# A routed expert kernel: the last group's row scatters lose their index copies, and in three-tile visits the next visit's rows are transposed one unit later

## The chip, the core and the metric

The kernel runs on one core of one Trainium2 chip. The metric is the device time of one execution in microseconds; lower is better. The engines that matter are PE (matrix multiply; PEld is its weight load), ACT and DVE (elementwise work), POOL (here mostly the issue of indirect DMAs) and SP (the issue of plain DMAs). They run from separate instruction queues, each in order, and wait for one another through semaphores. All DMAs of the core share 16 DMA engines.

## The reference

A convolution over 7 neighbouring positions with softmax weights makes 23040 token rows of 192 values. Each row is then routed to one of 4 groups and one of 4 experts in that group, goes through that expert's two-layer network, and is scaled.

```python
w = np.exp(weight_gen - max); w = w / (w.sum(-1) + 1e-9)         # B=8, S=2880, H=8, K=7
x = np.einsum('bshk,bskhg->bshg', w, x_unf).reshape(23040, 192)
g_idx = argmax(x @ w_group)                                       # 4 groups
e_idx = argmax(xg @ w_expert[g])                                  # 4 experts in each
h = np.maximum(xg @ w1[g, e], 0.0)                                # 192 -> 1024
out[tok] = g_w * e_w * (h @ w2[g, e])                             # 1024 -> 192
```

## The kernel before

The tokens pass in 15 groups of 12 x 128. For each group DVE makes the convolution, and the router gives each token a row number `posi` in a buffer `rows` in device memory, where each expert has a stretch of its own. `scatter_row` (L522) writes 128 rows of 194 values at a time with an indirect DMA that POOL issues, 12 of them a group (L527).

In the groups of `SPACED` each scatter first copies its 128 row numbers from `posi` into one of three small tiles `ix` (L526, a ring of three). A copy may run only when the scatter that last used its tile is done, so that no more than about three scatters are under way. In groups outside `SPACED` the scatter reads `posi` directly.

After the last group `table` also writes 16 fills of 256 padding rows (L599, `rows<-rem`), one for each expert's end. The results of the experts go out by indirect DMAs on the same POOL queue (L1049, `out<-y`). The order of POOL's instructions is set when the program is built, and POOL follows it strictly.

The experts' work is a list of visits: one visit loads one expert's weights and runs 1, 2 or 3 tiles of 128 rows through it (a cut visit has two and a half, or one and a half). A visit of two tiles has 4 units, a visit of three (`cur.wide`) has 8. The main loop of `blocks` (L1176) emits for each unit, in this order: the first product `gemm1` of unit u; for some u the preparation of the next visit; the second product `gemm2` of two units before, and after a visit's last unit `finish`, with its output copies `y` (L1038, ACT), and for cut visits `gemm2_half` (16 small products, L1022).

The preparation of the next visit `nxt` is `prep_x(nxt, 0)`: four transposes of two row tiles on PE into the tile `tpx` (L939, L940), a copy on ACT that rounds them (`xh`, L945), and on DVE the remainder (`xl`, L896, as all the delayed subtractions). When the next visit has a third tile, `prep_x(nxt, 2)` comes at unit 4, and in a three-tile visit it uses the same `tpx`, so it waits until `xl` has read it. Before the transposes ACT copies the last 64 columns of the rows to `xd` (L921).

Weights come in by SP: the first layer's as three loads into `raw` (L848, L855), the second layer's as one load of 768 KB (L859). In the round of six two-tile visits before the last round, and in the last round, the second layer is split into two parts: ACT rounds it to `wc` in two halves (L888), DVE makes the remainders, and there is a single `raw` buffer for it, so that the next load starts when the second half is done. In these visits DVE also makes the remainder of each hidden unit (`pr`, L896 as SCALAR_TENSOR_TENSOR), after ACT's `hh` (L979) and, in cut visits, ACT's copy of the half tile (L983).

The last round of visits, which needs the last group's rows, has 3 visits of three tiles, 7 of two and a half, 2 of two, 4 of one and a half and 2 of one. One further visit of three tiles stands in an earlier round, and there the second layer is not split.

Of the kernel before, what the change touches and what calls it, by code (L numbers as in the profile page):

```python
# [22 lines left out]
LATE = (1.0, 3.0, 3.0)  # L23
AHEAD = (1.0, 1.0, 2.5)
HURRY = 12
SPACED = range(2, 15)
HALVES = (36.0, 42.0, 48.0, 54.0, 60.0, 66.0, 72.0, 78.0)
WHOLE = 12
SINGLE = tuple((k,) for k in range(7))
# [13 lines left out]
def conv_moe_kernel(ctx: ExitStack, tc: tile.TileContext, x, wgen, w_group, w_expert, w1, w2, out):  # L43
# [221 lines left out]
    def run(eng, cost, *deps):  # L265
        clk[eng] = max([clk[eng]] + [d + HOP for d in deps]) + cost
        return clk[eng]
# [10 lines left out]
    def round_of(g):  # L278
        return next(r for r in range(NR) if g < ENDS[r])
# [170 lines left out]
    def ranks(g, o, ls, tls):  # L450
# [64 lines left out]
        for s in range(n):  # L515
            run("pool", 2.2 if g in SPACED else 1.28, clk["dve"])
            scatter_row(pi[:, s:s + 1], xrow[s // SC][:, s % SC, :], round_of(g), g in SPACED)
        if g + 1 in ENDS:
# [3 lines left out]
    def scatter_row(idx, src, r, spaced):  # L522
        ix = idx
        if spaced:
            ix = new_ix()
            nc.gpsimd.tensor_copy(out=ix, in_=idx)  # L526
        written_once(nc.gpsimd.indirect_dma_start(  # L527
            out=rows[:, :], out_offset=bass.IndirectOffsetOnAxis(ap=ix, axis=0),
            in_=src, in_offset=None, bounds_check=NROW - 1, oob_is_err=False), r)
# [272 lines left out]
    def ready(n):  # L802
        return order[n][:2] in arrive

    def plain(n):
        return order[n][1] == 1
# [101 lines left out]
    def flush():  # L908
        for q in (late, held):
            while q:  # L910
                q.pop(0)()
        held.extend(later)
        later[:] = latest
        latest.clear()

    def prep_d(b):
        if b.plain:
            return
        b.xd = new_xd()[:, 0:b.nt]
        b.td = run("act", 0.1 + 0.13 * b.nt, b.o.tx)  # L920
        nc.scalar.copy(out=b.xd, in_=b.x[:, :, P:D].unsqueeze(2).broadcast_to([P, b.nt, 2, HP]))  # L921
# [112 lines left out]
    def finish(b):  # L1034
        for t in range(b.nt - b.cut):
            gate = b.x[:, t, D:D + 1]
            y = new_y()
            nc.scalar.activation(out=y, in_=b.acc[t], func=AF.Copy, scale=gate)  # L1038
            ty = run("act", 0.3, b.ty)
            after(ty, 0.0 if b.o.whole else 0.35, None, send, b, t, y)  # L1040
# [27 lines left out]
    def units_of(n):  # L1068
        return NFT if tiles_of(order[n][1]) == 3 else NU
# [6 lines left out]
    def blocks(n0, n1, paced):  # L1076
        want, jobs = [], []

        def pump(upto=None):
            for a in list(want):  # L1080
                if a[1] == 0 and upto is None and ready(a[0]) and arrive[order[a[0]][:2]] > max(clk["pe"], clk["dve"]):
                    continue
                if upto is not None and a[0] <= upto:
                    need(a[0])
                if not ready(a[0]) or a not in want:
                    if upto is None:
                        break
                    continue
                want.remove(a)
                load(*a)  # L1090
# [10 lines left out]
        def ask_w(n):  # L1101
            ask(n, 1)
            ask(n, 2)
# [17 lines left out]
        def block(i):  # L1121
            n = units[i][0]
            o = visits[n]
            b = Slot()
            b.th = {}
            b.plain, b.nt = plain(n), tiles_of(order[n][1])
            b.wide = b.nt == 3
            b.cut = o.cut
            if b.cut:
                b.hq = freed("xrow", 5, 2, [P, NFT, HB])  # L1130
            b.nv = 1 if b.wide else 2
            b.n = rows_of[order[n][1]]
            b.o, b.h, b.x = o, {}, o.xb
            b.clears = n == nmain - 4
            if not b.plain:
                while state["open"]:
                    assert step() is not False
                state["slots"] = True
            if not o.whole:
                state["starve"] = True  # L1140
                while step() is not False:
                    pass
                state["starve"] = False
            return b
# [24 lines left out]
        cur = block(0)  # L1169
# [6 lines left out]
        for i in range(len(units) + LAG):  # L1176
            if i < len(units):
                n, u = units[i]
                last = units_of(n) - 1
                gemm1(cur, u)  # L1180
                queue.append((cur, u))
                nxt_at = i + last + 1 - u
                if nxt_at < len(units):
                    if u == 0:
                        pump(units[nxt_at][0])
                        nxt = block(nxt_at)
                        prep_d(nxt)
                    if u == 1:
                        prep_x(nxt, 0)
                    if nxt.nt > 2 and u == (last // 2 + 1 if cur.wide else 1):  # L1190
                        prep_x(nxt, 2, not cur.wide)
                if u == last and i + 1 < len(units):
                    cur = nxt
            asks = []
            if i >= LAG:
                b, u = queue.pop(0)
                gemm2(b, u)
                if u == units_of(units[i - LAG][0]) - 1:
                    finish(b)
                    if b.cut:  # L1200
                        gemm2_half(b)
                    if i - LAG + 1 < len(units):
                        asks.append(units[i - LAG][0] + 3)
            if i < len(units):
                n, at = units[i]
                end = at == last
                if end and n + 4 < n1 and plain(n + 3) and not plain(n + 4):
                    ask_w(n + 4)
                    ask_w(n + 3)
                elif end and n + 3 < n1 and plain(n + 3):  # L1210
                    ask_w(n + 3)
                elif end and n + 4 < n1 and plain(n + 2):
                    ask_w(n + 4)
                did = 0
                for job in list(jobs):
                    m, part, h = job
                    if m > n + 2 or (part == 3 and (m > n + 1 or at < LAG)):
                        continue
                    must = end and m == n + 1
                    if not must and (did >= 1 or (m, part) in want or not ready(m)):  # L1220
                        continue
                    jobs.remove(job)
                    work_split(job)
                    did += 1
                state["unit"] += 1
                state["gemm"] += 1
            flush()
            if paced:
                fill(clk["pe"] + AHEAD[0 if cur.plain else 1 if cur.o.whole else 2])
            for a in asks:  # L1230
                ask_x(a)
            pump()
# [45 lines left out]
```

## Time and profile before

| | |
|---|---|
| median of 3 runs | 1198.86 us (1195.1 to 1199.44) |
| the profiled execution | 1187.8 us, span 1185.8 us |
| PE busy | 1116.4 us (94% of the span) |
| DVE busy | 950.8 us (80%) |
| ACT busy | 649.0 us (55%) |
| POOL busy | 579.9 us (49%) |
| bytes moved | 275.11 MB, 232 GB/s over the span |

The busy times are of the profiled execution. It took 11.1 us less than the median of the runs shown; nothing here says where those 11 us lie. Times of rows below are microseconds from the start of the span.

### The profile page before, as it was taken

What the parts mean: (1) busy time and instruction counts of PE and PEld (TensorE: products, weight loads), DVE (VectorE), ACT (ScalarE), POOL (GpSimd) and SP (SyncE); (2) the same over time, 40 slices, a digit from 0 to 9 for tenths busy, and PEclk for the clock granted to TensorE, in tenths of its full rate; (3) what the DMA queues carried; (4) which work ended last, traced back from release to release, by engine and by line L of the source; (5) the groups of instructions that cost most, each with busy time, mean ns of one, the idle gap of its engine ahead of it and who ended that gap; (6) DMA issues with size and microseconds to landing.
All of it is one profiled execution on the core that took longest, in us unless ns stands there. A gap on an engine that the chain in (4) does not pass through costs nothing.

```text
span 1185.8 us, 24775 instructions
## 1 busy us (share of the span) xinstructions
PE 1116.4 (94%) x8357; PEld 1047.3 (88%) x8357; DVE 950.8 (80%) x1682; ACT 649.0 (55%) x1307; POOL 579.9 (49%) x613
## 2 busy tenths in 40 slices
PE   5787998999999999999999999999799899999997
PEld 2444988999999999998989999999799899999997
DVE  8899997989998989998988989898464576665661
ACT  1341435555565555665556566565446676666772
POOL 7164284647275745765563837284736421222221
PEclk9998999999999999999999999999999999999999
DMA  5798999887878777878795868767748875556562
GB/s 173 212 310 231 305 310 289 247 276 232 279 228 280 243 256 231 277 224 285 218 304 179 275 214 269 256 197 211 225 134 240 261 243 171 172 182 181 179 208 73
DMA packets 84345, 275.11 MB, mean 232 GB/s; under 512 B 15296, under 2 KB 34160, under 8 KB 82416
## 3 DMA queue, kind: packets, MB, share of 16 engines
q1 hardware_dynamic: 64056, 229.77, 62.3%
q0 software_dynamic: 20032, 43.39, 11.9%
q8 instruction: 67, 1.10, 0.4%
q14 instruction: 70, 0.57, 0.1%
q10 hardware_dynamic: 120, 0.28, 0.1%
HBM read 225.83 MB, written 47.88 MB: 231 GB/s over the span
## 4 chain that ended last, share of the span: by engine, by line
PE 65%; issue 15%; DVE 6%; DMA 4%; POOL 3%; ACT 3%; another core or an unknown queue 2%; SPq 0%; POOLq 0%; ACTq 0%; DVEq 0%
PE py L1011 27%; PE ph L965 27%; POOL out L1049 3%; DVE pr L317 3%; PE pl L399 2%; DMA raw<-in_moe_w 1%; PE tpx L940 1%; PE tpx L939 1%; PE ph L358 1%; PE py L1013 1%; DMA xb<-rows 1%; DVE pr L353 1%; PE tp L416 1%; PE pl L416 1%
## 5 line engine op out<-in xcount | busy, mean ns | idle before, releaser
L965 PE MATMUL ph<-xh,wa 128*128 128x256 f32 (+3 forms) x1992 | 455.0, 303 | 0.4 <-issue 0.3
L1049 POOL DMA_INDIRECT out<-y,xb x189 | 213.8, 1131 | 421.7 <-ACT y L1038 182.6
L1011 PE MATMUL py<-wc,hh 128*128 128x192 f32 x2160 | 400.9, 326 | 2.1 <-ACT y L1038 1.9
L965 PE MATMUL ph<-xl,wa 128*128 128x256 f32 (+3 forms) x1328 | 350.7, 285 | 1.0 <-DVE xl L896 0.6
L1011 PEld LDWEIGHTS py<-wc,hh 128*128 128x128 f32 x2160 | 345.5, 190 | 3.4 <-ACT y L1038 2.6
L965 PEld LDWEIGHTS ph<-xh,wa 128*128 128x128 f32 x1992 | 336.4, 190 | 6.5 <-issue 4.9
L974 ACT ACTIVATE hh<-ph 128x512 f32<-128x512 f32 (+2 forms) x296 | 165.8, 560 | 265.9 <-PE ph L965 233.2
L965 PEld LDWEIGHTS ph<-xl,wa 128*128 128x128 f32 x1328 | 251.6, 189 | 2.3 <-issue 1.1
L317 DVE TENSOR_TENSOR pr<-xin,wt 128x1152 f32<-128x1152 f32 x186 | 249.0, 1350 | 4.2 <-PE py L358 3.7
L527 POOL DMA_INDIRECT rows<-xrow,ix x156 | 222.2, 1425 | 47.3 <-POOL ix L526 32.9
L335 DVE TENSOR_TENSOR xrow<-xrow,pr 128x1152 f32<-128x1152 f32 x144 | 194.6, 1351 | 0.7
L896 DVE SCALAR_TENSOR_TENSOR pr<-ph,hh 128x256 fp32r<-128x256 f32 (+2 forms) x128 | 65.8, 514 | 87.4 <-ACT hh L979 44.3
L896 DVE TENSOR_TENSOR wa<-raw,wa 128x1024 fp32r<-128x1024 f32 x83 | 101.3, 1220 | 29.3 <-ACT wa L872 19.0
L526 POOL COPY ix<-posi 128x1 int32<-128x1 int32 x156 | 72.9, 479 | 73.3 <-DMA rows<-xrow,ix 39.2
L1013 PE MATMUL py<-wc,hh 128*128 128x384 f32 x320 | 101.8, 362 | 0.0
L979 ACT ACTIVATE hh<-ph 128x256 fp32r<-128x256 f32 (+2 forms) x128 | 59.1, 462 | 57.4 <-PE ph L965 55.2
L872 ACT CAST wa<-raw 128x1024 fp32r<-128x1024 f32 x83 | 87.2, 1050 | 0.0
L881 ACT CAST wa<-raw 128x1024 fp32r<-128x1024 f32 x83 | 86.5, 1043 | 0.0
L1014 PE MATMUL py<-wc,pr 128*128 128x192 f32 x320 | 80.5, 252 | 0.0
L1038 ACT ACTIVATE y<-py,xb 128x192 f32<-128x192 f32 x175 | 66.5, 426 | 20.5 <-PE py L1011 15.9
L896 DVE TENSOR_TENSOR xl<-tpx,xh 128x512 fp32r<-128x512 f32 (+1 forms) x92 | 59.2, 644 | 12.0 <-ACT xh L945 10.7
L1014 PEld LDWEIGHTS py<-wc,pr 128*128 128x128 f32 x320 | 61.5, 192 | 0.0
(205 smaller groups left out, 1341.6 us busy)
## 6 DMA issues: line engine op xcount, KB each, us to landing
wc<-in_moe_w SPq DMA_DIRECT2D x73, 768.0 KB
raw<-in_moe_w SPq DMA_DIRECT2D x83, 512.0 KB
xin<-in_x SPq DMA_DIRECT2D x14, 1728.0 KB
raw<-in_moe_w SPq DMA_DIRECT2D x91, 256.0 KB
raw<-w1lo SPq DMA_DIRECT2D x83, 256.0 KB
xb<-rows SPq DMA_DIRECT2D x75, 194.0 KB
wa<-in_moe_w SPq DMA_DIRECT2D x24, 384.0 KB
raw<-in_moe_w SPq DMA_DIRECT2D x11, 768.0 KB
```

Source lines behind the costliest of these rows:

```text
L317: nc.vector.tensor_tensor(out=dst, in0=o.xin[:, c0 + k:c0 + k + SC, :].rearrange("p s (h g) -> p s h g", g=HG), in1=w4[:, c0:c0 + SC, :, k ...
L335: nc.vector.tensor_tensor(out=acc, in0=acc, in1=prs[k - 2], op=ALU.add)
L527: written_once(nc.gpsimd.indirect_dma_start(out=rows[:, :], out_offset=bass.IndirectOffsetOnAxis(ap=ix, axis=0), in_=src, in_offset=None, ...
L872: nc.scalar.copy(out=o.wa[:, 0, :], in_=o.raw[0])
L881: nc.scalar.copy(out=o.wa[:, 2, :], in_=o.raw[1])
L896: f(*a, **k)
L965: nc.tensor.matmul(ph[:, v, :], lhsT=w[:, f0:f0 + P], rhs=rhs, start=i == 0, stop=i == len(terms) - 1)
L974: nc.scalar.activation(out=hh, in_=ph, func=AF.Relu)
L1011: nc.tensor.matmul(b.acc[t], lhsT=hh[:, v, c], rhs=wc[0][:, f, :], start=f == 0 and not (b.wide and t == 1), stop=f == NFT - 1 and not (b. ...
L1013: nc.tensor.matmul(b.py[t], lhsT=hh[:, v, c], rhs=wc[f // 4][:, f % 4].rearrange("p l d -> p (l d)"), start=f == 0, stop=False)
L1014: nc.tensor.matmul(b.acc[t], lhsT=hl[:, v, c], rhs=wc[f // 4][:, f % 4, 0, :], start=False, stop=f == NFT - 1)
L1049: ins = nc.gpsimd.indirect_dma_start(out=out[:, :], out_offset=bass.IndirectOffsetOnAxis(ap=b.x.bitcast(I32)[part, t, D + 1:D + 2], axis=0 ...
```

## The change

Group 14, the last, leaves `SPACED`: its 12 scatters read `posi`, and the 12 copies to `ix` are gone. In visits of three tiles `prep_x(nxt, 0)` comes after unit 2's first product, not after unit 1's.

```diff
-SPACED = range(2, 15)
+SPACED = range(2, 14)
...
-                    if u == 1:
+                    if u == (2 if cur.wide else 1):
                         prep_x(nxt, 0)
```

POOL, at the last group's scatters, before (`rows<-xrow,ix` is a scatter, `rows<-rem` a fill, `out<-y` an output; a TENSOR_LOAD reads the place of a fill):

```order
486 L526 COPY ix_177<-posi 128x1
487 L526 COPY ix_178<-posi 128x1
488 L526 COPY ix_176<-posi 128x1
489 L527 DMA rows<-xrow,ix_177 188928x194
490 L527 DMA rows<-xrow,ix_178 188928x194
491 L527 DMA rows<-xrow,ix_176 188928x194
492 L597 TENSOR_LOAD pfi
493 L597 ISA x2
494 L599 ISA
495 L599 DMA rows<-rem 256x1x194
496 L526 COPY ix_177<-posi 128x1
```

and of the changed kernel at the same place:

```order
485 L1049 DMA out<-y_190,xb 23040x192
486 L527 DMA rows<-xrow,posi 188928x194 x12
487 L1049 DMA out<-y_191,xb 23040x192
488 L1049 DMA out<-y_192,xb 23040x192
489 L597 TENSOR_LOAD pfi
490 L597 ISA x2
491 L599 ISA
492 L599 DMA rows<-rem 256x1x194
```

Before, the scatters, fills and two outputs are mixed over some ninety rows, and the last eight fills stand behind a second pair of outputs. After, the 12 scatters stand together, then come two outputs, eight fills, two outputs, eight fills, and the outputs that are left.

ACT, in a visit of two and a half tiles in the last round, before:

```order
1035 L979 ACTIVATE hh<-ph_13653 128x256
1036 L983 ACTIVATE xrow<-ph_13653 128x64
1037 L945 CAST xh_181<-tpx 128x2x256
1038 L1038 ACTIVATE y_185<-py_13523,xb 128x192
1039 L1038 ACTIVATE y_186<-py_13524,xb 128x192
1040 L1038 ACTIVATE y_187<-pl,xb 128x192
1041 L881 CAST wa<-raw_195 128x1024
1042 L979 ACTIVATE hh<-ph_13703 128x256
1043 L983 ACTIVATE xrow<-ph_13703 128x64
1044 L888 CAST wc<-xin 128x4x192
1045 L979 ACTIVATE hh<-ph_13734 128x256
```

and of the changed kernel:

```order
1037 L1038 ACTIVATE y_185<-py_13511,xb 128x192
1038 L1038 ACTIVATE y_186<-py_13512,xb 128x192
1039 L1038 ACTIVATE y_187<-pl,xb 128x192
1040 L881 CAST wa<-raw_195 128x1024
1041 L979 ACTIVATE hh<-ph_13685 128x256
1042 L983 ACTIVATE xrow<-ph_13685 128x64
1043 L945 CAST xh_181<-tpx 128x2x256
1044 L888 CAST wc<-xin 128x4x192
1045 L979 ACTIVATE hh<-ph_13721 128x256
```

The copy `xh` has moved behind the outputs, the weight copy `wa` and unit 2's `hh`. DVE in the same visit, before:

```order
1443 L896 SCALAR_TENSOR_TENSOR pr<-ph_13703,hh 128x256
1444 L896 TENSOR_TENSOR wa<-raw_193,wa 128x1024
1445 L896 TENSOR_TENSOR xl_183<-tpx,xh_181 128x2x256
1446 L896 SCALAR_TENSOR_TENSOR pr<-ph_13734,hh 128x256
1447 L896 TENSOR_TENSOR wc<-xin,wc 128x4x192
```

and of the changed kernel:

```order
1443 L896 SCALAR_TENSOR_TENSOR pr<-ph_13685,hh 128x256
1444 L896 TENSOR_TENSOR wa<-raw_193,wa 128x1024
1445 L896 SCALAR_TENSOR_TENSOR pr<-ph_13721,hh 128x256
1446 L896 TENSOR_TENSOR xl_183<-tpx,xh_181 128x2x256
1447 L896 TENSOR_TENSOR wc<-xin,wc 128x4x192
```

The subtraction `xl` has changed places with unit 3's `pr`. This swap stands in each of the 10 visits of three tiles of the last round. On PE the four transposes move behind the second products of the visit before and behind unit 2's first product. SP's order does not change.

## Rows read from the trace of the kernel before

**Rows 1.** Windows (us): busy time (instructions) by engine, PE clock, DMA share, GB/s.

```profile
916.00:932.00 16.00, 14.07 (x111) 13.87 (x110) 7.65 (x12) 7.47 (x13) 10.86 (x13) 1.00 1.01 294
932.00:948.00 16.00, 13.97 (x96) 13.78 (x97) 11.13 (x17) 12.63 (x23) 2.93 (x3) 0.89 0.72 217
```

**Rows 2.** Timeline of PE: start, duration, instruction, idle time before and its releaser.

```profile
932.55 0.33 PE L939 MATMUL tpx<-ident,xb 128*128 128x128 f32 x1 [2.48 <-issue]
934.36 0.33 PE L940 MATMUL tpx<-ident,xd 128*128 128x128 f32 x1 [1.48 <-ACT xd L921]
```

**Rows 3.** Timeline of ACT, 915 to 934 us.

```profile
915.79 0.84 ACT L888 CAST wc<-raw 128x768 fp32r<-128x768 f32 x1 [1.56 <-DMA raw<-in_moe_w]
...
931.47 0.83 ACT L888 CAST wc<-raw 128x768 fp32r<-128x768 f32 x1 [7.57 <-DMA raw<-in_moe_w]
...
933.90 0.40 ACT L921 COPY xd<-xb 128x256 f32<-128x256 f32 x1
```

**Rows 4.** Timeline of SP's queue: two loads of second-layer weights.

```profile
910.52 0.34 SPq L859 DMA_DIRECT2D raw<-in_moe_w  x1
...
920.46 0.34 SPq L859 DMA_DIRECT2D raw<-in_moe_w  x1
```

**Rows 5.** Timeline of PE: first transpose of the next visit, in four-unit visits.

```profile
920.26 0.27 PE L939 MATMUL tpx<-ident,xb 128*128 128x128 f32 x1
...
945.56 0.27 PE L939 MATMUL tpx<-ident,xb 128*128 128x128 f32 x1
...
955.22 0.27 PE L939 MATMUL tpx<-ident,xb 128*128 128x128 f32 x1
```

**Rows 6.** Timeline of POOL, from the last group's first scatter on.

```profile
876.83 0.98 POOL L527 DMA_INDIRECT rows<-xrow,ix  x1 [0.33 <-POOL ix L526]
...
893.68 0.18 POOL L526 COPY ix<-posi 128x1 int32<-128x1 int32 x1 [2.75 <-DMA rows<-xrow,ix]
...
909.89 0.77 POOL L599 DMA_DIRECT2D rows<-rem  x1
...
915.34 2.22 POOL L599 DMA_DIRECT2D rows<-rem  x3
...
923.70 0.68 POOL L599 DMA_DIRECT2D rows<-rem  x1 [0.59 <-issue]
924.68 1.97 POOL L1049 DMA_INDIRECT out<-y,xb  x1 [0.31 <-issue]
...
930.84 0.97 POOL L1049 DMA_INDIRECT out<-y,xb  x1 [0.30 <-DMA rows<-rem]
```

**Rows 7.** Timeline of POOL: first and twelfth scatter of group 1, unspaced.

```profile
91.36 1.05 POOL L527 DMA_INDIRECT rows<-xrow,posi  x1 [8.90 <-DVE units L552]
...
107.22 0.98 POOL L527 DMA_INDIRECT rows<-xrow,posi  x1 [0.30 <-issue]
```

**Rows 8.** Timelines of PE, ACT and DVE in a visit of two and a half tiles.

```profile
1044.39 0.27 PE L939 MATMUL tpx<-ident,xb 128*128 128x128 f32 x1
...
1044.75 0.42 PE L1013 MATMUL py<-wc,hh 128*128 128x384 f32 x1
...
1051.02 0.33 PE L939 MATMUL tpx<-ident,xb 128*128 128x128 f32 x1 [0.51 <-issue]
...
1045.41 0.61 ACT L945 CAST xh<-tpx 128x512 fp32r<-128x512 f32 x1
1045.88 0.78 ACT L1038 ACTIVATE y<-py,xb 128x192 f32<-128x192 f32 x2
...
1049.67 0.21 ACT L983 ACTIVATE xrow<-ph 128x64 f32<-128x64 f32 x1
...
1048.81 0.42 DVE L896 SCALAR_TENSOR_TENSOR pr<-ph,hh 128x256 fp32r<-128x256 f32 x1 [0.90 <-ACT xrow L983]
1049.15 1.22 DVE L896 TENSOR_TENSOR wa<-raw,wa 128x1024 fp32r<-128x1024 f32 x1
1050.29 0.68 DVE L896 TENSOR_TENSOR xl<-tpx,xh 128x512 fp32r<-128x512 f32 x1
```

## Prediction

> **What bounds the kernel now.** I read the page first: PE is busy for 94% of the span, so time can only be won where PE stands still or runs slowly, or where it does work that can go. The change removes no work of PE's. So the question is where PE stands still near the two places that the change touches, and who is late there.
>
> The windows by stage come second. Around the last group's scatters one stretch stands out [rows 1]: from 916 to 932 the DMA engines are full (share 1.01, 294 GB/s), and PE loses 1.93 us of 16; from 932 to 948 it loses 2.03 us more, and its granted clock is 0.89 on average there, so that part of that stretch ran at the lower of its two levels.
>
> Third, the timeline of PE in that stretch. PE ends its last product at 932.55 - 2.48 = 930.07, begins a transpose of the next visit at 932.55, and then waits 1.48 us for ACT's `xd` [rows 2]. ACT shows why `xd` is late: it stood still for 7.57 us until a load of second-layer weights had landed, then did `wc` at 931.47 and came to `xd` only at 933.90 [rows 3]. SP had issued that load at 920.46 [rows 4]. So it took 931.47 - 920.46 = 11.0 us; the same load one visit before, issued at 910.52, was used at 915.79, after 5.3 us [rows 3, 4].
>
> What did the wait cost in all, the slow clock after it included? In undisturbed visits the first transpose returns after 955.22 - 945.56 = 9.66 us [rows 5]. From 920.26 to 945.56, two visits, it took 25.30 us. The loss is 25.30 - 2 x 9.66 = **5.98 us**. This is the largest thing near the change.
>
> Fourth, who filled the DMA engines: POOL's timeline [rows 6]. The last group's scatters begin at 876.83 and are still held back by the index ring at 893.68 (a copy waited 2.75 us for a scatter to end). So the fills come late: eleven of the sixteen are issued from 909.89 to 923.70, the last seven of them from 916.1 on (the second of the three at 915.34 starts there). The outputs come later still: seven `y` scatters from 924.68 to 930.84. These fall on the very load that was late.
>
> **Part one, the scatters.** Removed are 12 small copies on POOL and the waits of the ring. The copies themselves cost nobody but POOL, which is busy 49%. What moves is the DMA traffic behind them. Unspaced scatters were issued in group 1 at (107.22 - 91.36) / 11 = 1.44 us each [rows 7]. Twelve from 876.83 end at about 894.1. The two outputs behind them cost about 1.3 us each (0.98 of work and about 0.3 of gap, as the scatters show [rows 6]), to 896.7. The fills went at one in about 1.14 us: from 909.89 to 923.70 lie ten steps and two outputs, so (13.81 - 2.4) / 10. Sixteen fills and two more outputs need 18.3 + 2.6 us, to about 917.6, where before the last fill started at 923.70. Then the outputs that have piled up, two pairs by then, go until about 923.
>
> So between 916.2 and 931.5 POOL issues one or two fills and about six outputs. Before it issued seven fills and seven outputs. A fill is 256 x 194 x 4 = 199 KB, an output 128 x 192 x 4 = 98 KB: some 2.1 MB before, 0.8 to 1.0 after. At 294 GB/s the 1.2 MB less are 4.1 us. The load issued at 920.46 then lands after 11.0 - 4.1 = 6.9 us, at 927.4, if nothing else speeds it up; at the 5.3 us of its neighbour at 925.8.
>
> When is it early enough? From the landing to the end of `xd` it took 934.30 - 931.47 = 2.83 us, and PE wants it one transpose after 930.07, at 930.2 or so; so up to 927.4 costs nothing. My two estimates of the landing are at and below that edge. I take a rest of 0.4 us for it, with no fall of the clock. Bounds: nothing is won if the landing doesn't move; 5.98 us if it comes in time.
>
> Does the traffic harm someone where it now goes? Loads between 876 and 916 have long leads: of second-layer weights there is only the one at 910.52, and the fills it meets until 917.6 are as dense as those that it met before (909.89 and the three from 915.34 are of the same pace [rows 6]), when it landed in 5.3 us and PE did not wait. That is the cover; if it went, the same 5.98 us would be lost one visit earlier. The last round's row loads wait for all scatters and fills, and the outputs' tiles come free after their scatters; both now end earlier than before, so nothing is late there.
>
> The Trainium skill, "DMA: Bandwidth & Descriptors", section "Queues, rings and completion order", says that each DMA engine goes round robin among the queues that have work, a packet at a time, so that an unthrottled POOL queue takes its turns from SP's loads. This speaks against taking the throttle away, but the rows show that what hurts is which load meets the traffic. By the rule alone the wait would only move, which is the first rival below.
>
> **Part two, the transposes.** In the ten three-tile visits of the last round the four transposes move, and with them `xh` on ACT and `xl` on DVE. No instruction is added. PE does the same work; what can change is the wait of the third tile's transpose for `xl`: it is 0.51 us, and begins at 1051.02 right behind `xl`, which ran from 1050.29 for 0.68 us [rows 8]. So any lateness of `xl` goes straight to PE. `xl` now stands behind unit 3's `pr`, which costs 1049.15 - 1048.81 = 0.34 us of DVE, and which must wait for ACT's work on unit 3, whose last piece ends at 1049.67 + 0.21 = 1049.88.
>
> On ACT `xh` costs 1045.88 - 1045.41 = 0.47 us. It used to stand ahead of the outputs, now it stands ahead of unit 3's `hh`. Taken alone that would not change when unit 3's `hh` runs, since both places are ahead of it; but in between ACT waits for PE's half-tile products, and those come earlier by what the four transposes took, 1044.75 - 1044.39 = 0.36 us. So unit 3's last piece ends at 1049.88 - 0.36 + 0.47 = 1049.99. DVE's `wa` starts 0.36 us earlier too, and is done by 1050.0. `pr` runs at about 1050.02, `xl` at 1050.36 in place of 1050.29: 0.07 us later. The long wait that `xl` had before, from the end of `xh` at 1046.02 to 1050.29, is the room in which the move is hidden. Nine visits have a third tile to prepare: 9 x 0.07 = **0.6 us lost**. Bounds: nothing; or, if the 0.36 us are not given back and `pr` comes in full, 0.47 + 0.34 = 0.81 a visit, 7.3 us. A gain I exclude, since one more instruction stands ahead of `xl`. The one earlier visit of three tiles has no third tile behind it to wait.
>
> The sum is made against the profiled execution: 1187.8 - 5.98 + 0.4 + 0.6 = 1182.8, which is 5.0 us less. The median of the runs shown is 1198.86, and I take the 5.0 us off that: **1193.9 us**. The 11.1 us between the two are in no row. If a part of them is more of the same wait, the gain is larger; I allow it to double, 1187.
>
> **Rivals.** (1) The wait only moves: the crowd of scatters and fills now makes the load of 910.52 land after 11 us, at 921.5, and PE loses its 5.98 us a visit earlier. For it: the DMA engines have little to spare already before 916. Against: the load met the same fills before. Time: 1198.86 + 0.6 = 1199.5. (2) Slower: `xl` comes late in every three-tile visit, because ACT is busy without a gap there and `xh` pushes unit 3's `hh`. The price is 9 x 0.81 = 7.3 us, and it decides from 0.6 us a visit on, where 5.98 - 0.4 is eaten up: 1198.86 - 5.6 + 7.3 = 1200.6. Against: the 0.36 us that PE's products come earlier. (3) The fills are not what made the load late, or only half: SP's own loads queued ahead of it are. Half the loss stays: 1198.86 - 3.0 + 0.6 = 1196.5. (4) The change doesn't do what it says: that is out for the scatters, since the copies are gone, and their ring with them.
>
> **How the numbers follow.** The forecast has 0.64, the rivals (1) 0.14, (2) 0.12, (3) 0.10. Half a percent is 6.0 us, about what can be told from no change here. My 5.0 us lie just inside. Of the forecast's 0.64 somewhat more than half, 0.37, goes beyond 6.0 us, since the rest of 0.4 may be nothing and the longer runs may hold a longer wait; rivals (1) and (3) end within the bound. Rival (2) passes it only if `xl` is late by (5.6 + 6.0) / 9 = 1.3 us a visit, that is, if `pr` waits longer for unit 3 than I priced: I give that half of its 0.12, and 0.02 more to a second late load behind the first in (1). Faster 0.37, same 0.55, slower 0.08. The range goes from 1187 to rival (2)'s 1200.6, rounded up to 1201; the forecast's own is 1190 to 1196.
>
> **What would show it.** Right: PE has no wait near 930, its clock stays full from 916 to 948, and the load of second-layer weights that was used after 11.0 us takes 5 to 7. POOL's 12 scatters stand 1.3 to 1.5 us apart, and the last fill starts near 917. The third tile's transpose still waits 0.5 to 0.6 us in the visits of two and a half tiles. Wrong: a wait of ACT for `raw` over 7 us somewhere from 900 to 935, or a wait for `xl` near 1.3 us in each of the nine visits.

## The result and the profile after

The changed kernel is slower: 1209.82 us median (1206.88 to 1214.65, 6 runs) against 1195.0 us of the kernel before beside it (6 runs); ratio 1.012, 95% interval 1.0088 to 1.0152. The profiled execution took 1206.88 us, its span is 1204.8 us. The forecast was 1193.9 us, in a range from 1187 to 1201, and a slower kernel had a chance of 0.08. Ratios in this document leave slow executions out, and of the traces only that of `straight, paced` below is of a slow one.

The wait at which the change aimed is gone from this trace. Windows of the changed kernel, columns as in [rows 1], first the stretch of the last group's scatters, then the two that answer to [rows 1]:

```profile
884.00:900.00 16.00, 5.82 (x44) 5.62 (x43) 9.53 (x56) 3.02 (x5) 11.67 (x12) 0.74 0.62 195
900.00:916.00 16.00, 13.58 (x76) 13.08 (x77) 7.18 (x41) 6.95 (x13) 7.45 (x10) 0.72 0.67 188
916.00:932.00 16.00, 16.00 (x120) 16.00 (x119) 2.88 (x3) 9.15 (x16) 9.79 (x12) 1.00 0.98 280
932.00:948.00 16.00, 16.00 (x126) 16.00 (x125) 9.83 (x15) 11.91 (x21) 3.39 (x4) 1.00 0.65 215
```

From 916 to 948 PE has no gap and its granted clock is 1.00, though the DMA engines are as full (0.98) as before. But from 884 to 900 PE works for only 5.82 us of 16, and its clock falls to 0.72 to 0.74 on average, so that after its stand it ran in part at 1.2 GHz, the lower of its two levels. So the loss now lies some 30 us earlier, and it is larger.

The load that had been late answers to [rows 3, 4] so (SP's queue, then ACT, then PE's first transposes as in [rows 5]):

```profile
943.84 0.34 SPq L859 DMA_DIRECT2D raw<-in_moe_w  x1
```

```profile
948.19 0.84 ACT L888 CAST wc<-raw 128x768 fp32r<-128x768 f32 x1 [0.92 <-DMA raw<-in_moe_w]
```

```profile
943.63 0.27 PE L939 MATMUL tpx<-ident,xb 128*128 128x128 f32 x1
...
953.29 0.27 PE L939 MATMUL tpx<-ident,xb 128*128 128x128 f32 x1
```

It is used 4.35 us after its issue, where it took 11.0, and the visit lasts 953.29 - 943.63 = 9.66 us, as an undisturbed one. POOL's timeline answers to [rows 6]:

```profile
884.37 0.97 POOL L527 DMA_INDIRECT rows<-xrow,posi  x1 [3.84 <-DVE units L552]
885.65 0.98 POOL L527 DMA_INDIRECT rows<-xrow,posi  x1 [0.30 <-issue]
...
898.42 0.97 POOL L527 DMA_INDIRECT rows<-xrow,posi  x1 [0.30 <-issue]
...
905.04 0.73 POOL L599 DMA_DIRECT2D rows<-rem  x1 [0.42 <-issue]
...
927.74 0.68 POOL L599 DMA_DIRECT2D rows<-rem  x1 [1.14 <-issue]
```

Twelve scatters stand (898.42 - 884.37) / 11 = 1.28 us apart. The last fill starts at 927.74, not near 917 as forecast; before it was 923.70 [rows 6]. What PE and ACT do meanwhile, each in its own timeline:

```profile
887.09 0.27 PE L940 MATMUL tpx<-ident,xd 128*128 128x128 f32 x1
887.20 1.47 PE L1011 MATMUL py<-wc,hh 128*128 128x192 f32 x8
...
889.54 0.28 PE L965 MATMUL ph<-xl,wa 128*128 128x256 f32 x1
900.60 1.01 PE L1011 MATMUL py<-wc,hh 128*128 128x192 f32 x2 [10.78 <-issue]
903.42 2.29 PE L1011 MATMUL py<-wc,hh 128*128 128x192 f32 x6 [1.82 <-ACT y L1038]
```

```profile
888.74 0.60 ACT L974 ACTIVATE hh<-ph 128x512 f32<-128x512 f32 x1 [2.36 <-PE py L1011]
893.00 0.58 ACT L945 CAST xh<-tpx 128x512 fp32r<-128x512 f32 x1 [3.66 <-remote]
900.12 0.42 ACT L1038 ACTIVATE y<-py,xb 128x192 f32<-128x192 f32 x1 [6.54 <-remote]
902.95 0.42 ACT L1038 ACTIVATE y<-py,xb 128x192 f32<-128x192 f32 x1 [2.41 <-remote]
```

`xh` needs PE's transposes alone. They end at 887.09 + 0.27 = 887.36, and ACT is free from 889.34, but `xh` runs at 893.00. The product that `y` reads ends at 887.20 + 1.47 = 888.67, and `y` runs at 900.12. PE in turn cannot start the next product until `y` has emptied `py`. PE and ACT stand; the word that a result is ready arrives late. The chain of waits of that stretch finds no producer ("remote" in a row is the same):

```profile
889.34 3.64 another core or an unknown queue
...
893.02 7.08 another core or an unknown queue
...
900.15 2.78 another core or an unknown queue
```

DVE shows it between its own small instructions, which wait 0.4 to 0.6 us for one another here, while the same three start 0.1 us apart at 886.50 and again at 888.69:

```profile
896.72 0.16 DVE L620 TENSOR_REDUCE ri<-past 128x1 f32<-128x16 f32 x1
897.29 0.18 DVE L622 TENSOR_TENSOR tv<-tv,first 128x16 f32<-128x16 f32 x1 [0.41 <-DVE ri L620]
897.99 0.15 DVE L623 TENSOR_SCALAR tab<-ri 128x1 int32<-128x1 f32 x1 [0.52 <-DVE tv L622]
```

I call this late signals below. It shows from the fourth of POOL's twelve scatters on (`xh` could have run at 889.34), and its last row, at 902.95, is 3.6 us behind the end of the twelfth (898.42 + 0.97).

### The profile page after: what moved, and what is told of

Read it like the earlier page. It is cut to its first block, busy times and chain, and to the rows that moved or that the text cites. A ratio compares the mean times of both kernels' runs of the same rounds, so it can differ in the third digit from the quotient of the medians.

```text
span 1204.8 us, 24762 instructions
## 1 busy us (share of the span) xinstructions
PE 1120.2 (93%) x8357; PEld 1051.3 (87%) x8357; DVE 951.4 (79%) x1682; ACT 649.6 (54%) x1307; POOL 568.8 (47%) x601
## 4 chain that ended last, share of the span: by engine, by line
PE 66%; issue 16%; DVE 5%; another core or an unknown queue 3%; POOL 3%; ACT 3%; DMA 3%; SPq 0%; POOLq 0%; DVEq 0%; ACTq 0%
PE py L1011 27%; PE ph L965 27%; POOL out L1049 3%; DVE pr L317 2%; PE pl L399 2%; DMA raw<-in_moe_w 2%; PE tpx L940 1%; PE ph L358 1%; PE tpx L939 1%; PE py L1013 1%; PE tpx L358 1%; PE tp L416 1%; PE py L358 1%; DMA xin<-in_x 1%
## 5 line engine op out<-in xcount | busy, mean ns | idle before, releaser
L1011 PE MATMUL py<-wc,hh 128*128 128x192 f32 x2160 | 403.5, 328 | 15.8 <-issue 10.9
L1011 PEld LDWEIGHTS py<-wc,hh 128*128 128x128 f32 x2160 | 347.5, 191 | 18.1 <-issue 12.4
L527 POOL DMA_INDIRECT rows<-xrow,ix x144 | 208.0, 1444 | 42.8 <-POOL ix L526 31.1
L526 POOL COPY ix<-posi 128x1 int32<-128x1 int32 x144 | 66.2, 471 | 65.8 <-DMA rows<-xrow,ix 35.6
L872 ACT CAST wa<-raw 128x1024 fp32r<-128x1024 f32 x83 | 87.2, 1051 | 0.0
```

Of the source, the lines that this page charges most:

```text
L527: written_once(nc.gpsimd.indirect_dma_start(out=rows[:, :], out_offset=bass.IndirectOffsetOnAxis(ap=ix, axis=0), in_=src, in_offset=None, ...
L872: nc.scalar.copy(out=o.wa[:, 0, :], in_=o.raw[0])
L1011: nc.tensor.matmul(b.acc[t], lhsT=hh[:, v, c], rhs=wc[0][:, f, :], start=f == 0 and not (b.wide and t == 1), stop=f == NFT - 1 and not (b. ...
```

## Where the time went, visit by visit

A visit's length is here the time from one cast of first-layer weights (ACT L872) to the next one's. "Early" is the visit after the three-tile one in the earlier round (the 55th to the 56th such cast; before: 799.33 to 811.72), "burst" the one in which the last group's scatters begin (877.25 to 888.15), "load" the one of the late load (918.93 to 934.20). "Four" is the sum of four visits: the one ahead of "load", "load" itself and the two behind it (before: 909.00 to 953.9). Up to about 799 us nearly all these kernels run the same instructions. After the first comparison the runs were made in five batches, each on one chip with the kernel before beside it; the last column is the ratio to that.

| kernel | batch, before's median | early | burst | load | four | ratio (95%) |
|---|---|---|---|---|---|---|
| before | first | 12.4 | 10.9 | 15.3 | 44.9 | |
| before again | 4, 1193.3 | 12.1 | 10.9 | 12.0 | 42.8 | 0.9978 (0.9946 to 1.0009) |
| changed | first, 1195.0 | 15.8 | 26.5 | 9.7 | 38.9 | 1.0120 (1.0088 to 1.0152) |
| changed, again | 2, 1194.09 | 12.6 | 24.5 | 9.7 | 38.9 | 1.0122 (1.0091 to 1.0152) |
| changed, third | 4, 1193.3 | 17.0 | 23.0 | 9.7 | 38.9 | 1.0086 (1.0056 to 1.0117) |
| changed, fourth | 5, 1191.47 | 14.5 | 21.9 | 9.7 | 38.9 | 1.0091 (1.0060 to 1.0123) |
| part one alone | 1, 1191.46 | 12.4 | 23.6 | 9.7 | 38.9 | 1.0057 (1.0036 to 1.0077) |
| part two alone | 1, 1191.46 | 17.1 | 10.9 | 14.6 | 44.2 | 1.0014 (0.9987 to 1.0040) |
| copies without ring | 1, 1191.46 | 12.4 | 21.7 | 9.7 | 38.9 | 1.0033 (1.0012 to 1.0054) |
| straight, paced | 1, 1191.46 | 12.6 | 10.3 | 13.7 | 42.5 | 0.9984 (0.9954 to 1.0013) |
| straight, short pause | 5, 1191.47 | 12.1 | 14.3 | 10.0 | 42.5 | 1.0003 (0.9975 to 1.0031) |
| burst in group 13 | 2, 1194.09 | 12.5 | 11.1 | 13.8 | 45.3 | 0.9993 (0.9969 to 1.0017) |
| paced outputs | 2, 1194.09 | 24.5 | 10.1 | 14.7 | 52.4 | 1.0446 (1.0400 to 1.0492) |
| fills between | 2, 1194.09 | 12.4 | 10.4 | 9.6 | 41.0 | 0.9995 (0.9963 to 1.0027) |
| 24 of half the rows | 4, 1193.3 | 12.4 | 37.9 | 9.4 | 38.9 | 1.0210 (1.0173 to 1.0247) |
| 24 of half the width | 4, 1193.3 | 12.6 | 38.0 | 10.0 | 38.9 | 1.0175 (1.0144 to 1.0206) |
| part one, with part two in the last round | 3, 1169.02 | 12.0 | 10.4 | 10.0 | 42.8 | 1.0000 (0.9983 to 1.0018) |
| part one, with part two before it | 3, 1169.02 | 12.0 | 10.4 | 8.6 | 41.4 | 0.9990 (0.9972 to 1.0008) |
| 24 of half the rows | 3, 1169.02 | 12.0 | 10.3 | 13.0 | 44.5 | 1.0008 (0.9987 to 1.0029) |
| 24 of half the width | 3, 1169.02 | 12.0 | 10.3 | 14.9 | 46.9 | 1.0024 (1.0006 to 1.0042) |

From the trace of before to the first one of the changed kernel: early 15.8 - 12.4 = +3.4, burst 26.5 - 10.9 = +15.6, load 9.7 - 15.3 = -5.6, the first three-tile visit of the last round +1.2 (16.3 for 15.1), all further visits up to the 82nd cast together +0.2 (142.1 for 141.9). The sum is +14.8 us. The two spans differ by 19.0; of the rest, 3.7 lie before 799 us. That the medians differ by 1209.82 - 1195.0 = 14.8 as well is chance, since each stands for six executions and the sum for one of each.

The column "four" says more of the late load than "load" does. It is 38.9 us in the eight traces whose burst visit is ten us or more too long, and 41.0 or more in all others. In the changed kernel the last fill starts 4.6 us before the four visits begin (927.74 against 932.37), in before 14.7 us behind their begin (923.70 against 909.00). Of these 19.3 us the fills account for 4.1, since they end that much sooner after the burst visit's begin (42.4 us for 46.5); the rest is the stand of the burst, which made the visits late. In the other seven traces with 38.9 us the last fill starts between 6.3 us ahead of that begin and 3.0 us behind it. Its place is not all, though: with fills between it starts 0.4 us ahead, and the four take 41.0. No kernel without the stand has lost the whole wait.

## The experiments

The edits are shown by their decisive lines.

**Each part alone.**

```diff
-SPACED = range(2, 15)
+SPACED = range(2, 14)
```
```diff
-                    if u == 1:
+                    if u == (2 if cur.wide else 1):
```

> Part one alone. Theory A (twelve scatters that POOL issues back to back, 1.28 us apart, make the signals of PE, ACT and DVE arrive late, some 13 us in all): slower by 10 to 18 us, ratio 1.008 to 1.015, and a stand of PE of 8 us or more inside or just behind the burst. Rival B (the moved transposes are the cause): 5 us faster to no change, ratio 0.995 to 1.002, no such stand.

> Part two alone. Theory A: within 3 us of before, ratio 0.9975 to 1.0025, and the wait of PE near 930 is still there. Rival B: slower by 10 to 18 us, ratio 1.008 to 1.015.

Part one: 1.0057, with stands of PE of 7.1 and 2.5 us in the burst. Theory A holds in kind; the ratio and the longest stand are below the 1.008 and the 8 us that it named. Part two: 1.0014, not to be told from no change; rival B falls. Its early visit took 17.1 us in place of 12.4, though.

**The pace or something beside it.** One kernel keeps the copies but takes the ring away, the other keeps the pace without ring and copies. In both, PE, ACT, DVE and SP keep the order of before to the row.

```diff
-            ix = new_ix()
+            ix = new_ix() if mine is None else mine
```

(`mine` is a column of its own for each scatter of group 14.)

```diff
-        ix = idx
+        ix, _ = idx, None if old is None else tc.keep_in_program_order(nc.gpsimd.memset(old, 0.0))
```

(`old` is, in group 14 alone, a tile of convolution weights that nobody reads any more.)

> The last group's row numbers are still copied, but each into a column of its own, so that nothing holds a scatter back; PE, ACT, DVE and SP keep the order of before to the row. Theory A: slower by 8 to 18 us, ratio 1.007 to 1.015, with a wait of ACT of 5 us or more put down to an unknown queue behind the burst's start. Rival C (not the burst, but the other order that the planner gives PE, ACT, DVE and SP when it prices a scatter at 1.28 in place of 2.2): no wait there, and 5 us faster to no change, ratio 0.995 to 1.002.

> The last group's scatters read their row numbers straight, but POOL clears an old 128x672 tile ahead of each, which nobody reads any more, so that they stand about 2.2 us apart; PE, ACT, DVE and SP keep the order of before. Theory A: no wait of ACT over 5 us put down to an unknown queue from 875 to 905; the fills come earlier than before or at the same time; time from 6 us faster to 3 us slower, ratio 0.995 to 1.0025. Rival D (reading the row numbers where DVE wrote them is what hurts, not the pace): slower by 8 us or more, ratio over 1.007.

Without the ring the burst visit takes 21.7 us though the copies are there and no other engine's order is changed: rival C falls. (The ratio, 1.0033, is below what A named. ACT waits 11.96 us in one piece with no known releaser, where A asked for 5; PE's own gaps are short there.) With the pace it takes 10.3 us though the row numbers are read straight: rival D falls. POOL in the paced kernel, scatters 1.81 us apart:

```profile
889.03 0.97 POOL L527 DMA_INDIRECT rows<-xrow,posi  x1 [0.17 <-issue]
890.00 0.68 POOL L523 MEMSET wt<- 128x672 f32 x1
890.84 0.97 POOL L527 DMA_INDIRECT rows<-xrow,posi  x1 [0.16 <-issue]
```

Its last fill came at 931.7, 11.7 us behind the begin of the four visits, and they take 42.5 us: with late fills the load is late too, which fits the prediction's reading of it. "Pace" and "pause" mean here that POOL does something else between two DMAs; it does not rest.

**The changed kernel again, the burst in group 13, fills between the scatters, and paced outputs.**

```diff
-            scatter_row(pi[:, s:s + 1], xrow[s // SC][:, s % SC, :], round_of(g), g in SPACED)
+            scatter_row(pi[:, s:s + 1], xrow[s // SC][:, s % SC, :], round_of(g), g in SPACED and g != 13)
```
```diff
+            if g == 14:
+                tc.keep_in_program_order(ins)
+                for _ in range(2 if s % 3 == 2 else 1):
+                    lay(early, round_of(g))
```

(`lay` issues the next of the 16 fills.)

```diff
+        ix = new_ix()[part, :]; nc.gpsimd.tensor_copy(out=ix, in_=b.x.bitcast(I32)[part, t, D + 1:D + 2])
```

> The changed kernel once more, beside the others. Theory A: part one alone cost 6.8 us and part two alone 1.6 us; if they add up, 8.4 us slower than before, ratio 1.005 to 1.009, with a wait of PE of 7 us or more behind the burst of scatters. If the two harm each other, as its first measurement has it, ratio 1.009 to 1.015.

> The burst is moved one group earlier: group 13 reads its row numbers straight and unspaced, group 14 is spaced as before; PE, ACT, DVE and SP keep the order of before. Theory A (any burst of scatters delays the signals of the other engines): a wait of PE or ACT of 4 us or more at group 13's scatters, near 780 to 805, and the wait near 930 as before; slower by 3 to 14 us, ratio 1.0025 to 1.012. Rival E (the stand belongs to the last group's place, with DVE's tables and the fills behind): no such wait, ratio 0.998 to 1.002.

> The last group's scatters read straight, and POOL issues a fill behind each (two behind every third), so that the scatters stand about 2.3 us apart with no clearing and the last fill is issued some 10 us earlier than before. Theory A with the prediction's reading of the late load: no stand behind the scatters, no wait near 930 either, 3 to 6 us faster, ratio 0.995 to 0.998. Rival (a fill counts in the burst like a scatter): a stand of 5 us or more, ratio over 1.003.

> The outputs' scatters get the same pace as the scatters of the groups: their row numbers are copied on POOL through the same ring of three. PE, ACT, DVE and SP keep the order of before. Theory A, taken wider (five outputs in a row are a burst as well): ACT's waits put down to an unknown queue, 34 us in sum before, fall below half, and the time by 4 to 15 us, ratio 0.987 to 0.997. Rival F (outputs that come later hold back the y tiles and the row loads): slower, ratio over 1.002.

The changed kernel repeated its loss: 1.0122. The burst in group 13 gave 0.9993 (0.9969 to 1.0017). Its trace has the stand, with ACT waiting

```profile
861.04 0.60 ACT L974 ACTIVATE hh<-ph 128x512 f32<-128x512 f32 x1 [5.27 <-remote]
```

and the visit in which this burst falls takes 18.2 us in place of 10.8; but the next takes 15.7 in place of 23.1, which before had a wait of its own of 8.03 us for a late signal. So it changed place, and rival E falls on the trace, not on the time. With fills between the scatters the burst's stand is gone (10.4), and of the late load a part is left: the visit ahead of "load" takes 13.0 us in place of 9.9, "four" is 41.0. From the visit before the burst on its trace is 4.1 us shorter than the first of before and 2.5 us shorter than the second, but the time is 0.9995, so that no gain is measured.

Paced outputs took the late signals away almost everywhere. ACT's waits with no known releaser, over the whole run, before (34.2 us) and there (3.1 us; 31.1 and 32.1 in the two other kernels of this batch that pace the last group):

```profile
ACT xT L435 <- remote: 20.4, 3, 8.0
ACT hh L974 <- remote: 13.8, 6, 3.7
```

```profile
ACT xd L921 <- DMA xb<-rows: 84.7, 12, 13.4
...
ACT hh L974 <- remote: 3.1, 2, 1.8
```

This speaks for the theory beyond the last group, with a reservation: a kernel that waits so long for rows leaves other waits less room to show. And it is a bad kernel: outputs and group scatters now share one ring, the rows come late (84.7 us of waits), and the time is 1.0446 (1.0400 to 1.0492). Rival F was right on the time, theory A on the waits.

**Which visits of part two, and what in a burst counts.** Part one, with part two in the last round alone, or in the earlier round alone (with `<` for `==`); and the twelve scatters cut into 24, by rows or by width.

```diff
-                    if u == 1:
+                    if u == (2 if cur.wide and order[n][0] == NR - 1 else 1):
```
```diff
+                scatter_row(pi[0:64, s:s + 1], xrow[s // SC][0:64, s % SC, :], round_of(g), False, rows[:, :])
+                scatter_row(own[0:64, s:s + 1], xrow[s // SC][64:P, s % SC, :], round_of(g), False, rows[:, :])
```
```diff
+                for k in range(2):
+                    scatter_row(own[:, k * n + s:k * n + s + 1], xrow[s // SC][:, s % SC, 97 * k:97 * k + 97], round_of(g), False, thin)
```

> Part one, and part two in the last round's visits alone. The changed kernel is 6 to 8 us slower than part one alone. Theory G (that rest is bound to the one earlier visit of three tiles, before 880): this kernel is like part one alone, ratio 1.004 to 1.008. Rival H (the last round's visits make it): ratio 1.009 to 1.014. In the last round's visits themselves at most 0.2 us each in either case.

> Part one, and part two in the one earlier visit of three tiles alone. Theory G: like the changed kernel, ratio 1.009 to 1.014. Rival H: like part one alone, ratio 1.004 to 1.008.

> Each of the last group's twelve scatters is split into two of 64 rows, read straight or from one copy, unspaced; PE, ACT, DVE and SP keep the order of before. Theory A1 (what delays the signals is the rate of rows): if a scatter of 64 rows still takes POOL about 1.28 us, rows come at half the rate, and there is no stand of PE over 3 us; ratio 0.995 to 1.002. Theory A2 (the number of scatters issued back to back counts): a stand of 13 us or more, ratio over 1.005.

> Each of the last group's twelve scatters is split into two of 128 rows of half the width (97 in place of 194 numbers), unspaced; PE, ACT, DVE and SP keep the order of before. Row by row the same rate as in the burst of twelve, for twice as long, but half the bytes in the same time. If rows count (A1): a stand of PE of 13 us or more, ratio over 1.005. If bytes count: no stand over 3 us, ratio 0.995 to 1.002.

All four fell on a chip where the kernel before takes 1169.02 us, 22 to 26 us less than elsewhere, and where no trace has a single wait of ACT without a known releaser. The first two are as fast as before, and G and H stay untold. What they show instead is the burst doing no harm. POOL, PE and ACT of the second, at the burst:

```profile
861.03 0.97 POOL L527 DMA_INDIRECT rows<-xrow,posi  x1 [0.30 <-issue]
862.30 0.97 POOL L527 DMA_INDIRECT rows<-xrow,posi  x1 [0.31 <-issue]
```

```profile
862.47 0.27 PE L940 MATMUL tpx<-ident,xd 128*128 128x128 f32 x1
862.57 1.47 PE L1011 MATMUL py<-wc,hh 128*128 128x192 f32 x8
```

```profile
862.89 0.58 ACT L945 CAST xh<-tpx 128x512 fp32r<-128x512 f32 x1
863.75 0.75 ACT L1038 ACTIVATE y<-py,xb 128x192 f32<-128x192 f32 x2 [0.28 <-PE py L1011]
```

The same 1.28 us apart, but `xh` runs 0.15 us after the transposes end (862.47 + 0.27), where the changed kernel had 5.64.

They also show what becomes of the late load when nothing stands in the burst. POOL's last fill, SP's load in the visit ahead of "load" and the cast that waits for it, in the first of the four:

```profile
895.65 0.68 POOL L599 DMA_DIRECT2D rows<-rem  x1 [0.50 <-issue]
```

```profile
891.17 0.34 SPq L859 DMA_DIRECT2D raw<-in_moe_w  x1
```

```profile
900.38 0.83 ACT L888 CAST wc<-raw 128x768 fp32r<-128x768 f32 x1 [5.50 <-DMA raw<-in_moe_w]
```

The fills end earlier among the visits than in before, 6.0 us behind the begin of the four in place of 14.7. But now they meet the load one visit earlier: it is used 900.38 - 891.17 = 9.2 us after its issue, that visit takes 13.5 us in place of 9.9, and the four take 42.8. (PE's own gap at its end, 1.79 us, is put down to the row load `xb`.) The wait has moved.

**The same question on other chips.** Before and changed kernel beside the two with 24 scatters; then a shorter pause (`nc.gpsimd.memset(old[:, 0:24, :], 0.0)`, 128x168 in place of 128x672), and the changed kernel a fourth time.

> The kernel before once more, for a trace on the same chip as the runs beside it. If signals come on time there (median of before near 1169 us): no wait of ACT put down to an unknown queue, 20 us shorter, and the wait near 930 shows whether it was there to be won. If they come late (median near 1192): about 34 us of such waits.

> The changed kernel a third time. Theory A2 (the burst costs time only on a chip where signals come late while POOL issues without a pause): median of before near 1192, then ratio 1.009 to 1.015 and a wait of PE of 7 us or more behind the burst; median of before near 1169, then ratio 0.996 to 1.001 and no such wait. Rival J (the changed kernel is slower on every chip): ratio over 1.005 in both.

> The twelve scatters split into 24 of 64 rows, once more. Where signals come late: no stand of PE over 3 us if the rate of rows decides (a scatter of 64 rows took POOL as long as one of 128), ratio 0.995 to 1.002; 13 us or more if the number of scatters does, ratio over 1.005. Where they come on time: 0.998 to 1.003 as in its first run.

> The twelve scatters split into 24 of half the width, once more. Where signals come late: a stand of PE of 13 us or more if rows decide, ratio over 1.005; no stand over 3 us if bytes decide, ratio 0.995 to 1.002. Where they come on time: 1.000 to 1.004 as in its first run.

> As the paced kernel, but POOL clears only a quarter of the old tile (128x168) ahead of each scatter of the last group, some 0.25 us, so that the scatters stand about 1.4 us apart, between the 1.28 of the burst and the 1.8 of the paced run. Where signals come late: a stand of PE of 8 us or more if 1.4 is still a burst (ratio over 1.004), none over 3 us if the pause itself is what counts (ratio 0.994 to 1.002). Where they come on time: 0.996 to 1.002.

> The changed kernel a fourth time, for a chip where signals come on time, if it is one: ratio 0.996 to 1.001 there by theory A2, over 1.005 by rival J. Where they come late: 1.008 to 1.014 as in its other runs.

Both chips had late signals. The changed kernel lost again (1.0086, 1.0091). Both kernels with 24 scatters stood twice as long: 37.9 and 38.0 us for the burst visit, 27 us over before, where the twelve of the changed kernel beside them added 23.0 - 10.9 = 12.1. A scatter of 64 rows takes POOL about as long as one of 128:

```profile
887.36 0.92 POOL L533 DMA_INDIRECT rows<-xrow,own  x1 [0.30 <-issue]
888.59 0.91 POOL L533 DMA_INDIRECT rows<-xrow,posi  x1 [0.30 <-issue]
```

So neither the rate of rows nor the bytes decide, but how many scatters POOL issues in a row, or for how long, which these runs do not tell apart: A2 holds, and A1 and the bytes fall. The short pause is between the two cases that were expected, near the second: its burst visit is 3.4 us longer (14.3 - 10.9), and PE's longest stand there is 0.9 us, with one clear of 0.26 us between scatters that stand 1.39 us apart:

```profile
887.25 0.97 POOL L527 DMA_INDIRECT rows<-xrow,posi  x1 [0.17 <-issue]
888.22 0.26 POOL L523 MEMSET wt<- 128x168 f32 x1
888.64 0.97 POOL L527 DMA_INDIRECT rows<-xrow,posi  x1 [0.17 <-issue]
```

A tenth of a microsecond in the pace takes two thirds of the burst's loss away (3.4 us in place of the 11.0 of the changed kernel beside it). Whether the slower pace or the other instruction between two DMAs does it, no run tells. No kernel tried here is measurably faster than before.

## Why the prediction was wrong

**The wait at 930.** The signs that I named came in part by luck. PE has no wait there, its clock is full, and the load is used after 4.35 us. But the last fill started at 927.74 in place of 917.6, and the load missed the fills because the burst had held the visits up. Where nothing held them up, rival (1) came true: "That is the cover; if it went, the same 5.98 us would be lost one visit earlier." It went. On the chip without late signals the load in the place of 910.52 is used after 9.2 and 8.6 us, and the four visits take 42.8 and 41.4 us with part one in place of the 38.9 of undisturbed ones. The two kernels take 1.0000 (from 0.9983 on) and 0.9990 (from 0.9972 on) of before's time there, which leaves no room for a gain of 5.0 us. (No trace of before was taken on that chip, and each of the two holds one half of part two.) Nor was the wait always 5.98 us: in the second trace of before the four visits take 3.9 us more than 38.9. One row I misread: from 924.68 to 930.84 there are five outputs, not seven. With five the traffic taken away is worth 3.4 us and not 4.1, and the load would have landed at 928.1, past the edge of 927.4.

**The step that failed**, and made the kernel slower, is in part one: "The copies themselves cost nobody but POOL, which is busy 49%. What moves is the DMA traffic behind them." Taking copies and ring away moved more than traffic: it took away the pauses between POOL's scatters. Without them the signals of the other engines came late; with pauses of 0.26 and 0.68 us they came little or not late. The price was +11.0 to +15.6 us in the burst visit over four traces, two to three times the 5.0 us that I hoped for. I asked of the scatters only whether DMA engines had room. They had: their share was 0.62 in 884 to 900. The rule of the Trainium skill that I weighed against the change (DMA: Bandwidth & Descriptors, section "Queues, rings and completion order": the engines go round robin among queues) was not what held PE up in the burst: the engines were a third idle, and the waits are for PE's results, not for loads. Of the load the traces without late signals agree with what I drew from it, that the wait only moves; the order of packets no run shows. Another sentence of the Trainium skill (Trainium Architecture — The Big Picture, "What this means for kernel authors") is that "A matmul on TensorE doesn't block a copy on VectorE unless you put a semaphore between them"; the trace agrees, as far as PE and ACT wait for each other only through such signals, and adds that one can come 5.64 us late.

I had a warning in the trace. In before ACT waits 34.2 us in all with no known releaser, 8.03 us of it in one piece, just behind six scatters and outputs that POOL issues 1.3 us apart. POOL's first and last of these, and ACT:

```profile
850.77 0.98 POOL L527 DMA_INDIRECT rows<-xrow,ix  x1 [0.56 <-issue]
857.22 0.97 POOL L1049 DMA_INDIRECT out<-y,xb  x1 [0.30 <-issue]
```

```profile
859.51 0.48 ACT L435 COPY xT<-pl 128x384 f32<-128x384 f32 x1 [8.03 <-remote]
```

A wait without a releaser near the change was a question, not noise. The rows that I took the pace from [rows 7] would not have warned me: ACT has no such wait up to 250 us, so none beside the unspaced scatters of the first two groups. Group 1's scatters stand 1.27 to 2.04 us apart, so that they too are not an unbroken row.

**Part two.** In the last round it costs 1.2 + 0.2 = 1.4 us in the first trace, where I said 0.6, so rival (2) was rightly low (the 0.2 answers to my 0.6, and part one alone already takes 15.9 us in the first of these visits, so that not all of the 1.2 need be part two's); the third trace has 19.3 us for the first of these visits in place of 15.1, which is 3 us more. But "The one earlier visit of three tiles has no third tile behind it to wait" looked at that visit alone, which is in fact 18.0 us for 17.9, and not at the one behind it. That is 15.0 us on average over the four traces of the changed kernel (17.1 with part two alone), where kernels without part two take 12.1 to 12.6 on chips with late signals, but for the one with paced outputs. No order was changed in it, but POOL reaches its five outputs sooner in the visit, and issues them without a pause; POOL and ACT of the changed kernel:

```profile
805.47 0.97 POOL L1049 DMA_INDIRECT out<-y,xb  x1 [0.30 <-issue]
806.74 0.98 POOL L1049 DMA_INDIRECT out<-y,xb  x1 [0.30 <-issue]
808.02 0.97 POOL L1049 DMA_INDIRECT out<-y,xb  x1 [0.30 <-issue]
```

```profile
811.85 0.48 ACT L435 COPY xT<-pl 128x384 f32<-128x384 f32 x1 [4.10 <-remote]
```

In before the first of the five outputs took 1.94 us, and ACT did not wait. In the second trace of the changed kernel POOL waited 1.29 us for ACT between the second output and the third; there ACT still waits 3.24 us, but PE does not, and the visit takes 12.6 us. That an unbroken row of outputs is the cause here too is argued; no run tested it on this visit. On the chip without late signals this visit is 12.0 us with part two and without.

**What stays open.** The parts alone add up to 0.71%, both together to 0.86 to 1.22%; the intervals of the two parts reach from 0.23 to 1.17%, and no run tells whether they harm each other. What made "four" 38.9 us is read from the places of the fills and loads; no run holds the visits up without a burst. The changed kernel itself has not run on the chip without late signals, only kernels with part one and half of part two. On which path the signals wait no run shows, nor whether the recording of events takes part in it.

**The 11.1 us** between the profiled execution and the median I allowed to be more of the wait near 930. No trace shows that, and differences of this size arise where neither part acts: kernels that are alike up to 799 us reach that mark between 799.33 and 812.21 us on the chips with late signals, and at 788.57 to 793.11 on the other.

## What to carry to other kernels

A copy or a ring ahead of an indirect DMA can be what keeps POOL from issuing without a break; before it is taken out, count how many DMAs would follow each other, and leave something between them (here a clear of 0.26 us brought the loss in the burst visit from 11 to 16 us down to 3.4). Read waits whose releaser the profile does not know together with POOL's timeline, and compare the end of the producer's row with the start of the consumer's. When a wait is gone, add up the visits on both sides of it, and ask whether the engine came later, not the load earlier. And time a change of this kind on more than one chip.

## What was not expected of the hardware

While POOL issues indirect DMAs one behind another, 1.28 us apart, results of PE, ACT and DVE that are done are taken up 0.5 to 11 us late; twelve in a row cost some 11 to 16 us, 24 some 27, while the DMA engines' share is 0.62 (884 to 900 in the changed kernel). This differs from chip to chip: the first comparison and four batches show it, one batch does not at all, and there the kernel before takes 1169.02 us in place of 1191 to 1195. The traces of the chips that show it also lack records: of ACT's 1269 counts of its signal the trace of before holds 1120, while the kernel with 24 scatters of half the width has all of its 1269 on the other chip.
